# Attention with a relative bias, LayerNorm and FFN on one core: three weight scales, a value bound from sums on ScalarE, a longer PSUM group, four fp32 visits

## The chip, the cores and the metric

The kernel runs on one core of a Trainium2 chip. The metric is the device time of one execution in microseconds (us). PE is TensorE, DVE is VectorE, ACT is ScalarE, POOL is GpSimd and SP is the engine that issues most DMAs; PEld is the loading of weights into TensorE.

## The reference

```python
# q, k, v: (4, 8, 576, 64); w1: (1, 32); w2: (32, 8)
scores = (1 / 8) * q @ k^T
rel    = |i - j|;  x = log1p(rel) / log1p(max(i, 1))
bias   = relu(x * w1 + b1) @ w2                    # (576, 576, 8), the same for every batch
attn   = softmax(scores + bias);  o = attn @ v
# o is laid out as (4, 576, 512)
xn  = (o - mean) / sqrt(var + 1e-6) * g_ln
out = o + relu(xn @ w_ch1) @ w_ch2                 # 512 -> 2048 -> 512
```

All inputs and the output are fp32.

## The kernel before, in words

**Units and visits.** The attention work is cut into 144 units. A unit is one head of 128 query rows (or, in the four tail visits, two heads of the last 64 rows). Units of one batch and one row block make a visit; there are 20 visits in the order of the table `ORD`: two tail visits (units 0 to 7), then (1, 0), (0, 0), (2, 0), (3, 0) with units 8 to 39, two more tail visits (40 to 47), and twelve visits of eight units. Visit (2, 0) holds units 24 to 31.

**One unit.** PE computes the scores in fp32 into PSUM (`sps`, line 394). One DVE instruction adds the bias tile `ldb` and takes the row maximum (line 418). ACT computes the exponential and its row sum (line 422). Then there are two ways to get the product with v:

- In a visit that stands in the set `NAT`, PE transposes the fp32 probabilities in five matmuls (`ptm`, `ptl`, lines 440 and 441), ACT copies them out of PSUM (lines 442 and 443), and PE multiplies with the raw fp32 values `vf` (line 490; line 507 in a tail visit).
- Otherwise ACT rounds the probabilities to fp16 (line 427), DVE computes the fp16 remainder (lines 446 and 448), a transposing DMA of SP turns both (line 451), and PE multiplies 14 times with the split values `v` (line 461).

The split values need a scale per batch and pair of heads: `v_max` takes the largest magnitude of `vf` on DVE (line 344), writes it to DRAM and reads it back to all partitions by two DMAs (`vmx`, `vall`, lines 348 and 350); `fin` reduces that on DVE (line 354) and rounds to a power of two; `split_v` makes the two fp16 halves (lines 369 and 372). When that happens follows from `uv`, the first unit of a batch that is not in a `NAT` visit.

**Weights.** The FFN weights arrive as 64-bit integers in 32 pieces (16 blocks f of 128 hidden columns, two matrices). DVE decodes each piece in three instructions (lines 612, 615, 617), PE adds up a Gram matrix per group of blocks (`gram`, line 626), `w_scale` makes a scale per group from it (lines 631, 633, 127 to 133, 637, 640), and `split_w` cuts each piece into two fp16 halves, one instruction on ACT (line 652) and one on DVE (line 655). A group is four blocks f, as `GROUPS` says.

**FFN.** It works on 18 row blocks k of 128 rows. A job is one row block with one group: 48 matmuls into `hps` (line 678), a ReLU split on ACT (line 683) and DVE (line 686), 12 matmuls into `y` (line 706), and one DVE instruction that adds `y`, scaled, to the row block x (line 717). Jobs are taken when their weights are split and their rows are normalised (`next_fs`); the variable `mbank` spreads them over the units.

**What sets the order.** A Python loop over the unit number u writes the steps; after it a scheduler puts the instructions of each engine in a fixed order when the program is built. Each engine then works its list off in order and waits where something is not there. Buffers come from pools: `ps_h` (one buffer, tag `h`) holds `hps`, and `ps_y` (one buffer each of tags `y0` and `y1`) holds `y` and `ptm`, or `gram` and some of the bias.

Of the kernel before, what the change touches and what calls it, by code (L numbers as in the profile page):

```python
# [22 lines left out]
def kernel(  # L23
# [50 lines left out]
    cb_sb = const.tile([128, 5], F32)  # L74
    one_sb = const.tile([2, 128], F32)
    gs_sb = const.tile([128, 512], F32)
    GROUPS = ((0, 4), (4, 8), (8, 12), (12, 16))
    NG = len(GROUPS)
    GOF = [g for g, (lo, hi) in enumerate(GROUPS) for _ in range(lo, hi)]
    half2 = const.tile([128, 2], F32)  # L80
    gram = {}
# [15 lines left out]
    ]  # L97
    vmx = [dram.tile([512], F32, name=f"vmx{b}") for b in range(NB)]
    wslot = [wp.tile([128, 1024], F32, name=f"w{f}") for f in range(NF - 1)]
# [129 lines left out]

    NAT = {(0, 4), (1, 4), (1, 0), (0, 0), (2, 0)}  # L230

# [109 lines left out]
    def v_max(b, g):  # L341
        if g == 0:
            vam[b] = small.tile([128, 4], F32, tag="vam", name="vam")
        red = V.tensor_reduce(out=vam[b][:, g:g + 1], in_=vraw[b, g], op=ALU.max, axis=AX.X,
                              apply_absolute_value=True)
        after(red, ttri[max(ttri)])
        if g == 3:
            SY.dma_start(out=vmx[b].rearrange("(p g) -> p g", g=4), in_=vam[b])
            all_ = ep.tile([128, EW], F32, tag="e", name="vall")[:, 0:512]
            SY.dma_start(out=all_, in_=vmx[b].partition_broadcast(128))  # L350

            def fin():
                ar = small.tile([128, 4], F32, tag="var", name="var")
                V.tensor_reduce(out=ar, in_=all_.rearrange("p (a g) -> p g a", g=4), op=ALU.max,
                                axis=AX.X)
                vsc[b] = small.tile([128, 4], F32, tag="vs", name="vs")
                pow2(ar, vsc[b], None)
                c8[b] = small.tile([128, NH], F32, tag="c8", name="c8")
                V.tensor_scalar(out=c8[b].rearrange("p (a b) -> p a b", b=2),
                                in0=vsc[b].unsqueeze(2).to_broadcast([128, 4, 2]),  # L360
                                scalar1=E_SCALE, scalar2=None, op0=ALU.mult)

            defer(lambda: defer(fin))

# [264 lines left out]
    def w_scale(g):  # L629
        f0, f1 = GROUPS[g]  # L630
        V.tensor_reduce(out=winv[:, g], in_=gram[g][:, 0:256].rearrange("p (a b) -> p a b", a=2),
                        op=ALU.max, axis=AX.X)
        G.tensor_tensor(out=winv[:, g], in0=winv[:, g], in1=half2, op=ALU.pow)

        def fin():
            wm = part_max(winv[:, g], 2, gram[g][:, 256:512])
            V.tensor_scalar(out=wred[:, g], in0=wm, scalar1=2.0 ** -5, scalar2=1e-20,
                            op0=ALU.mult, op1=ALU.max)
            pow2(wred[:, g], ws[:, g], winv[:, g])
            V.tensor_scalar(out=ycs[:, g:g + 1], in0=winv[:, g, 0:1], scalar1=winv[:, g, 1:2],  # L640
                            scalar2=ginv, op0=ALU.mult, op1=ALU.mult)
            wspl.extend((ff, ii) for ff in range(f0, f1) for ii in range(2))

        defer(fin)
# [46 lines left out]
    yq = []  # L691
    ydone = {}

    def ffn_w2(k, fs, hh):
        nt = len(blocks[k])
        n = 128 * nt
        g = GOF[fs[0]]
        f0, f1 = GROUPS[g]
        if fs[0] == f0:
# [8 lines left out]
        if fs[-1] == f1 - 1:  # L708
            for t in range(nt):
                yq.append((k, g, t, yps[k][t]))  # L710

    def ffn_y():
        while yq:
            k, g, t, y = yq.pop(0)
            b, c = tiles[blocks[k][t]]
            x = xt[b, c].rearrange("p a d -> p (a d)")
            V.scalar_tensor_tensor(out=x, in0=y, scalar=ycs[:, g:g + 1], in1=x,  # L717
                                   op0=ALU.mult, op1=ALU.add)
            ydone[k, t] = ydone.get((k, t), 0) + 1
            if ydone[k, t] == NG:  # L720
                if c < 4:
                    SY.dma_start(out=out[b, c * 128:c * 128 + 128, :], in_=x)
                else:
                    SY.dma_start(out=out[b:b + 2, 512:576, :], in_=x)

    jobs = [(k, g) for k in range(NBL) for g in range(NG)]
    cur_job = []
# [6 lines left out]
    def next_fs(u):  # L734
        if not cur_job:
            navail = sum(1 for a in avail_at if a <= u)
            for j in jobs:
                k, g = j
                if blocks[k][-1] < navail and wready_at.get(g, 1 << 30) <= u:
                    jobs.remove(j)  # L740
                    nf = 4 // len(blocks[k])
                    f0, f1 = GROUPS[g]
                    cur_job.extend((k, range(f, f + nf)) for f in range(f0, f1, nf))
                    break
# [41 lines left out]
    V.memset(one_sb, 1.0)  # L786
    V.memset(half2, 0.5)
    bias_setup()
# [42 lines left out]
    while u < NU + 6 or jobs or cur_job or pend or yq:  # L831
# [30 lines left out]
        for fn in todo.pop(u, []):  # L862
            fn()
        for g, (f0, f1) in enumerate(GROUPS):
            if wdone[0] >= 2 * f1 and g not in wready_at:
                wready_at[g] = u
        if u < NU + 9:
# [88 lines left out]
```

## Time and profile before

| | us |
|---|---|
| three runs | 700.3, 701.18, 702.73 |
| their median | 701.18 |
| the profiled execution | 697.11 |
| its span (first to last instruction) | 695.3 |
| PE busy in the span | 655.0 (94%) |
| DVE busy | 472.6 (68%) |
| ACT busy | 387.1 (56%) |

The profile shows one execution. It was 4.07 us shorter than the median of the runs, and 1.8 us of it lie outside the span. Durations below are read from that execution. A row of the timeline shows when an instruction (or a run of equal ones, with its count) started, how long it took, and in brackets how long its engine had been idle before and what ended that.

### The profile page before, as it was taken

To read this page: it belongs to the slowest core of one execution; us is meant where nothing else is said; L and a number is where in the kernel's file an instruction comes from. 1 tells how busy PE (TensorE), PEld (TensorE's weight loads), DVE (VectorE), ACT (ScalarE), POOL (GpSimd) and SP (SyncE) were. 2 spreads that over 40 slices of the span, in tenths; PEclk is the share of its full clock that TensorE was granted. 3 is DMA by queue.
4 is the path that set the end of the run, shared out by engine and by line. 5 is a ranking of instruction groups with operands and counts; after the bars stand their busy time and mean duration, and the time that the engine had idled before them with its cause. 6 is when DMAs were issued, how large, how long until landed. Compare 5 with 4: busy or idle time off the path is not lost.

```text
span 695.3 us, 18932 instructions
## 1 busy us (share of the span) xinstructions
PE 655.0 (94%) x7836; PEld 456.3 (66%) x7836; DVE 472.6 (68%) x1074; ACT 387.1 (56%) x762; POOL 81.8 (12%) x152
## 2 busy tenths in 40 slices
PE   6685888999999999999989999999999999999997
PEld 4343675786646676676657766766677677677774
DVE  6368989878237876869686766667676775767422
ACT  5765454647657745757585576767554554544110
POOL 3202132110000011101010110101000110000000
PEclk9888899789999999999999999999999999999999
DMA  8998794611238898886888978888896876738100
GB/s 311 284 402 310 248 311 152 187 49 35 66 85 183 153 261 161 171 181 146 169 158 188 234 166 163 169 159 185 166 242 138 173 145 136 131 70 131 35 17 15
DMA packets 180457, 116.17 MB, mean 167 GB/s; under 512 B 156180, under 2 KB 156308, under 8 KB 180372
## 3 DMA queue, kind: packets, MB, share of 16 engines
q1 hardware_dynamic: 169860, 79.96, 53.7%
q0 software_dynamic: 8640, 31.20, 14.2%
q10 hardware_dynamic: 1872, 3.81, 1.7%
q8 instruction: 61, 1.00, 0.6%
q14 instruction: 24, 0.20, 0.1%
HBM read 61.56 MB, written 15.64 MB: 111 GB/s over the span
## 4 chain that ended last, share of the span: by engine, by line
PE 67%; DMA 13%; DVE 11%; ACT 4%; issue 3%; SPq 1%; DVEq 0%; ACTq 0%
PE hps L678 24%; PE y L706 22%; PE sps L394 8%; PE xps L461 6%; DMA w<-in_w_ch_dram 4%; PE bps L182 3%; DMA ldb<-nb 2%; PE xps L490 2%; DMA nb<-ev 2%; DVE t L418 2%; DMA vall<-vmx 2%; DMA pt<-e 1%; DVE e L446 1%; DVE w L655 1%; DVE w L617 1%
## 5 line engine op out<-in xcount | busy, mean ns | idle before, releaser
L678 PE MATMUL hps<-xT,w 128*128 128x128 f16 x3240 | 195.9, 220 | 1.0 <-DVE w L655 0.8
L706 PE MATMUL y<-w,hh 128*128 128x512 f16 x810 | 188.3, 380 | 0.8 <-DVE x L717 0.8
L678 PEld LDWEIGHTS <-w 128*128 128x128 f16 x3240 | 185.3, 99 | 5.6 <-issue 1.8
L422 ACT ACTIVATE t<-t,m 128x576 f32<-128x576 f32 x144 | 110.8, 770 | 92.4 <-DVE m L418 92.1
L706 PEld LDWEIGHTS <-hh 128*128 128x128 f16 x864 | 79.9, 98 | 89.1 <-issue 3.8
L418 DVE CUSTOM_DVE_ANT_0 t<-sps,ldb 128x576 f32<-128x576 f32 x144 | 105.9, 750 | 22.8 <-DMA nb<-ev 7.6
L683 ACT ACTIVATE hh<-hps 128x512 f16<-128x512 f32 x72 | 42.8, 594 | 131.3 <-PE hps L678 125.8
L446 DVE SCALAR_TENSOR_TENSOR e<-t,e 128x512 f16<-128x512 f32 x112 | 77.1, 689 | 50.7 <-ACT e L427 50.7
L394 PE MATMUL sps<-kf,qf 64*128 64x288 f32 (+1 forms) x640 | 99.5, 444 | 8.6 <-DVE m L418 8.2
L686 DVE SCALAR_TENSOR_TENSOR hh<-hps,hh 128x512 f16<-128x512 f32 x72 | 49.6, 689 | 68.3 <-ACT hh L683 68.2
L461 PEld LDWEIGHTS <-pt 128*128 128x128 f16 (+1 forms) x1680 | 56.3, 100 | 40.9 <-issue 29.3
L427 ACT ACTIVATE e<-t 128x576 f16<-128x576 f32 x112 | 73.5, 675 | 2.4 <-DMA pt<-e 0.8
L717 DVE SCALAR_TENSOR_TENSOR x<-y,ycs,x 128x512 f32<-128x512 f32 x72 | 53.7, 746 | 25.6 <-PE y L706 25.6
L394 PEld LDWEIGHTS sps<-kf,qf 64*128 64x128 f32 (+1 forms) x640 | 49.3, 179 | 31.9 <-DVE m L418 8.5
L461 PE MATMUL xps<-v,pt 128*128 128x64 f16 (+1 forms) x1680 | 65.2, 194 | 2.8 <-DVE x L497 2.6
L292 POOL DMA_DIRECT2D kf<-in_k_s_dram x56 | 31.3, 560 | 115.6 <-PE sps L394 91.3
L161 ACT ACTIVATE r<-psi_sb,par_sb 128x448 f32<-128x448 f32 (+23 forms) x72 | 40.8, 615 | 6.2 <-DMA nb<-ev 3.5
L305 POOL DMA_DIRECT2D qf<-in_q_main_dram x32 | 18.0, 563 | 192.7 <-PE sps L394 167.9
L490 PE MATMUL xps<-vf,pt 128*128 128x64 f32 (+1 forms) x240 | 37.5, 290 | 0.0
L490 PEld LDWEIGHTS xps<-vf,pt 128*128 128x128 f32 (+1 forms) x240 | 33.5, 204 | 5.4 <-issue 2.7
L188 ACT ACTIVATE ev<-bps,cb_sb,par_sb 128x144 f32<-128x144 f32 (+27 forms) x48 | 26.0, 592 | 16.8 <-PE bps L182 16.8
L182 PE MATMUL bps<-r,nw_sb 128*32 128x448 f32 (+24 forms) x200 | 28.1, 494 | 0.7 <-ACT ev L188 0.5
(108 smaller groups left out, 599.3 us busy)
## 6 DMA issues: line engine op xcount, KB each, us to landing
kf<-in_k_s_dram POOLq DMA_DIRECT2D x56, 288.0 KB, 4.5
w<-in_w_ch_dram SPq DMA_DIRECT2D x23, 512.0 KB, 7.2
ldb<-nb SPq DMA_DIRECT2D x32, 288.0 KB, 4.7
qf<-in_q_main_dram POOLq DMA_DIRECT2D x32, 256.0 KB, 4.4
nb<-ev SPq DMA_DIRECT2D x24, 296.0 KB, 3.4
vf<-in_v_p_dram POOLq DMA_DIRECT2D x16, 320.0 KB, 7.1
out_dram<-x SPq DMA_DIRECT2D x18, 256.0 KB, 2.6
wend<-in_w_ch_dram SPq DMA_DIRECT2D x7, 512.0 KB, 6.4
```

Of the source, the lines that this page charges most:

```text
L182: T.matmul(out=flat[32 * s:32 * s + 32, a:b], lhsT=nw2_sb, rhs=rs[s][:, a:b], start=True, stop=True)
L394: T.matmul(out=o, lhsT=l, rhs=kk, start=True, stop=True, tile_position=(64 * hf, 64 * e))
L418: ttri[u] = V.tensor_tensor_reduce(out=halves(t), in0=ps[:, :, 0:HS], in1=halves(bias), scale=-0.125, scalar=3e38, op0=ALU.add, op1=ALU.mi ...
L422: S.activation(t, t, AF.Exp, bias=m, scale=-1.0, accum_out=l8[b, c][:, h:h + 1])
L427: S.activation(e16[:, 0:SEQ], t, AF.Copy, scale=E_SCALE)
L446: V.scalar_tensor_tensor(out=e16[:, 640:1152], in0=t[:, 0:512], scalar=E_SCALE, in1=e16[:, 0:512], op0=ALU.mult, op1=ALU.subtract)
L461: T.matmul(out=o, lhsT=p[:, m], rhs=v[:, j, a, :], start=(i == 0), stop=(i == len(ops) - 1))
L490: T.matmul(out=o[:, h, :], lhsT=p[0:n, 128 * j:128 * j + 128], rhs=vf[0:n, j], start=(j == 0), stop=(j == 4))
L678: T.matmul(out=h[:, idx * n:idx * n + n], lhsT=w[:, wo + kk * 128:wo + kk * 128 + 128], rhs=xT[k][:, xo + kk, 0:n], start=(i == 0), stop=( ...
L686: V.scalar_tensor_tensor(out=hh[:, 1], in0=h, scalar=0.0, in1=hh[:, 0], op0=ALU.max, op1=ALU.subtract)
L706: T.matmul(out=yps[k][t], lhsT=hh[:, a, o:o + 128], rhs=w[:, wo:wo + 512], start=(f == f0 and i == 0), stop=(f == f1 - 1 and i == 2))
L717: V.scalar_tensor_tensor(out=x, in0=y, scalar=ycs[:, g:g + 1], in1=x, op0=ALU.mult, op1=ALU.add)
```

## The change: four edits in one diff

- `GROUPS` has three groups instead of four: blocks f 8 to 15 share one scale, made when all eight are decoded. The three scales for `y` are used accordingly.
- For row blocks k of 4 and above, the `y` matmuls of f 8 to 15 (two jobs) add up in one PSUM tile, and x is updated once for both. For k below 4 each of the four jobs still updates x by itself.
- The bound for v is no longer a maximum. ACT sums the magnitudes of `vf` along each partition (`Abs` with an accumulated output), PE adds the 128 partial sums with a matmul by ones into a `ps_h` tile (`vps`), and DVE multiplies by 2^-13. The two DMAs through DRAM are gone.
- `NAT` loses visit (2, 0), so its eight units take the fp16 way, and `uv[2]` becomes 24 instead of 44: the values of batch 2 are loaded, bounded and split some 20 units sooner.

```diff
-    GROUPS = ((0, 4), (4, 8), (8, 12), (12, 16))
+    GROUPS = ((0, 4), (4, 8), (8, 16))
...
-    NAT = {(0, 4), (1, 4), (1, 0), (0, 0), (2, 0)}
+    NAT = {(0, 4), (1, 4), (1, 0), (0, 0)}
...
-        red = V.tensor_reduce(out=vam[b][:, g:g + 1], in_=vraw[b, g], op=ALU.max, axis=AX.X,
-                              apply_absolute_value=True)
+        sq = e16p.tile([128, 1152], F16, tag="e16", name="vab").bitcast(BF16)[:, 0:640]
+        red = S.activation(sq, vraw[b, g], AF.Abs, accum_out=vam[b][:, g:g + 1])
         after(red, ttri[max(ttri)])
         if g == 3:
-            SY.dma_start(out=vmx[b].rearrange("(p g) -> p g", g=4), in_=vam[b])
-            all_ = ep.tile([128, EW], F32, tag="e", name="vall")[:, 0:512]
-            SY.dma_start(out=all_, in_=vmx[b].partition_broadcast(128))
+            ps = ps_h.tile([128, 512], F32, tag="h", name="vps")
+            T.matmul(out=ps[:, 0:4], lhsT=one_sb, rhs=vam[b], start=True, stop=True)
+            ar = small.tile([128, 4], F32, tag="var", name="var")
 
             def fin():
-                ar = small.tile([128, 4], F32, tag="var", name="var")
-                V.tensor_reduce(out=ar, in_=all_.rearrange("p (a g) -> p g a", g=4), op=ALU.max,
-                                axis=AX.X)
+                V.tensor_scalar(out=ar, in0=ps[:, 0:4], scalar1=2.0 ** -13, scalar2=None, op0=ALU.mult)
...
-            defer(lambda: defer(fin))
+            defer(fin)
...
-        f0, f1 = GROUPS[g]
+        f0, f1 = GROUPS[g] if k >= 4 else (fs[0], fs[-1] + 1)
...
-                yq.append((k, g, t, yps[k][t]))
+                yq.append((k, g, t, yps[k][t], f1 == NF))
...
-            ydone[k, t] = ydone.get((k, t), 0) + 1
-            if ydone[k, t] == NG:
+            if last:
...
-    jobs = [(k, g) for k in range(NBL) for g in range(NG)]
+    jobs = [(k, qq) for k in range(NBL) for qq in range(4)]
...
-                    f0, f1 = GROUPS[g]
-                    cur_job.extend((k, range(f, f + nf)) for f in range(f0, f1, nf))
+                    cur_job.extend((k, range(f, f + nf)) for f in range(4 * g, 4 * g + 4, nf))
...
-        for g, (f0, f1) in enumerate(GROUPS):
-            if wdone[0] >= 2 * f1 and g not in wready_at:
-                wready_at[g] = u
+        for qq in range(4):
+            if wdone[0] >= 8 * qq + 8 and qq not in wready_at:
+                wready_at[qq] = u
```

The change moves instructions on every engine, since the scheduler starts anew. Line numbers of the new program are 3 or 4 lower.

PE, before, in units 26 and 27 of visit (2, 0): `t_2279` and `t_2348` are fp32 probabilities, `par_sb` holds the identity, `vf` the raw values.

```order
L440 MATMUL ptm_2355<-par_sb_109,t_2279 128x128 x4
L441 MATMUL ptl_2402<-par_sb_109,t_2348 64x128
L182 MATMUL bps_2594<-r_2573,nw2_sb_111 32x368
L182 MATMUL bps_2594<-r_2575,nw2_sb_111 32x368
L394 MATMUL sps_2649<-kf_2040,qf_2042 128x288 x2
L182 MATMUL bps_2594<-r_2577,nw2_sb_111 32x368
L182 MATMUL bps_2594<-r_2579,nw2_sb_111 32x368
L440 MATMUL ptm_2401<-par_sb_109,t_2348 128x128 x4
L490 MATMUL xps_2062<-vf_1458,pt_2354 128x64 x5
```

PE, after, where the first unit of that visit begins its product: `pt_1846` came from the transposing DMA, `v_1536` is a split value tile.

```order
L675 LDWEIGHTS w10_139
L675 MATMUL hps_1986<-xT_1095,w10_139 128x128
L458 LDWEIGHTS pt_1846
L458 MATMUL xps_1934<-v_1536,pt_1846 128x64
L458 LDWEIGHTS pt_1846
```

The five transposes and five fp32 products of a unit have left PE's list for these units, and 14 fp16 products stand there.

PE, before, at the first FFN matmuls that use weight block 8 (`w8`):

```order
L626 LDWEIGHTS wend_148
L626 MATMUL gram_1423<-wend_148 128x128
L490 MATMUL xps_1491<-vf_167,pt_1557 128x64 x4
L678 LDWEIGHTS w8_141
L678 MATMUL hps_1628<-xT_1091,w8_141 128x128
```

PE, after, at the same FFN matmuls; `vps` is the matmul by ones for batch 3:

```order
L702 MATMUL y0_1869<-w7_136,hh_1777 128x512
L348 MATMUL vps_1817<-vam_1580,one_sb_113 128x4
L487 MATMUL xps_1486<-vf_165,pt_1786 128x64
L675 LDWEIGHTS w8_137
L675 MATMUL hps_1986<-xT_1095,w8_137 128x128
```

Before, these FFN matmuls stand ahead of the scores of unit 26; now they stand behind the first two jobs of the next row block, behind the scores of unit 30, and right behind `vps`, whose PSUM buffer they take over.

DVE, before, between line 418 of unit 28 and of unit 29, where the last group of weights is split (`vs_1952` is the value scale of batch 3):

```order
L640 TENSOR_SCALAR ycs_119<-winv_118,ginv_122 128x1
L372 SCALAR_TENSOR_TENSOR v_2614<-vf_1511,vs_1952,v_2614 128x10x64
L655 SCALAR_TENSOR_TENSOR w12_145<-w13_146,ws_117,w12_145 128x512 x2
L686 SCALAR_TENSOR_TENSOR hh_1887<-hps_1838,hh_1887 128x512
L655 SCALAR_TENSOR_TENSOR w13_146<-w14_147,ws_117,w13_146 128x512 x2
L717 SCALAR_TENSOR_TENSOR x_1436<-y0_1921,ycs_119,x_1436 128x512
L497 TENSOR_TENSOR x_1967<-xps_1491,rl_1964 128x512
L655 SCALAR_TENSOR_TENSOR w14_147<-wend_148,ws_117,w14_147 128x512 x2
```

DVE, after, between the same two units:

```order
L637 TENSOR_SCALAR ycs_119<-winv_118,ginv_122 128x1
L652 SCALAR_TENSOR_TENSOR w8_137<-w9_138,ws_117,w8_137 128x512
L713 SCALAR_TENSOR_TENSOR x_1437<-y0_1821,ycs_119,x_1437 128x512
L652 SCALAR_TENSOR_TENSOR w8_137<-w9_138,ws_117,w8_137 128x512
L652 SCALAR_TENSOR_TENSOR w9_138<-w10_139,ws_117,w9_138 128x512 x2
L652 SCALAR_TENSOR_TENSOR w10_139<-w11_140,ws_117,w10_139 128x512 x2
L652 SCALAR_TENSOR_TENSOR w11_140<-w12_141,ws_117,w11_140 128x512 x2
L713 SCALAR_TENSOR_TENSOR x_1437<-y0_1869,ycs_119,x_1437 128x512
L352 TENSOR_SCALAR var_1819<-vps_1817 128x4
L494 TENSOR_TENSOR x_1904<-xps_1486,rl_1901 128x512
L652 SCALAR_TENSOR_TENSOR w12_141<-w13_142,ws_117,w12_141 128x512
```

The splits of blocks 8 to 11 have moved here from units 22 to 24, ahead of those of block 12 and up, and the reading of `vps` stands behind them; before, no value scale is read here.

## Rows read from the trace of the kernel before

**Rows 1.** Page, busy time, share and instructions of each engine
```profile
PE 655.0 (94%) x7836; PEld 456.3 (66%) x7836; DVE 472.6 (68%) x1074; ACT 387.1 (56%) x762; POOL 81.8 (12%) x152
```

**Rows 2.** Windows: stretch, length, busy PE, PEld, DVE, ACT, POOL, PEclk, DMA share, GB/s
```profile
144.00:181.30 37.30, 36.84 (x322) 24.65 (x322) 27.94 (x65) 23.52 (x46) 4.35 (x8) 1.00 0.22 61
181.30:237.30 56.00, 54.20 (x550) 35.58 (x549) 31.01 (x71) 38.11 (x77) 2.29 (x4) 1.00 0.58 120
300.00:380.00 80.00, 76.08 (x951) 51.11 (x948) 60.73 (x136) 53.90 (x106) 9.46 (x17) 1.00 0.77 162
380.00:640.00 260.00, 260.00 (x3375) 185.01 (x3372) 178.77 (x416) 145.64 (x288) 26.62 (x52) 1.00 0.80 161
```

**Rows 3.** Timeline of PE in visit (2, 0): fp32 transposes and products
```profile
182.01 0.30 PE L441 MATMUL ptl<-par_sb,t 128*64 128x128 f32 x1
182.24 0.43 PE L490 MATMUL xps<-vf,pt 64*128 64x64 f32 x2
...
186.70 0.61 PE L440 MATMUL ptm<-par_sb,t 128*128 128x128 f32 x4
187.15 1.36 PE L490 MATMUL xps<-vf,pt 128*128 128x64 f32 x10
188.44 0.89 PE L182 MATMUL bps<-r,nw_sb 128*32 128x416 f32 x4
```

**Rows 4.** Timeline of PE in a later visit: fp16 products
```profile
303.96 0.58 PE L461 MATMUL xps<-v,pt 128*128 128x64 f16 x14
304.38 2.84 PE L678 MATMUL hps<-xT,w 128*128 128x128 f16 x48
```

**Rows 5.** Groups of instructions by line over the span
```profile
L717 DVE SCALAR_TENSOR_TENSOR x<-y,ycs,x 128x512 f32<-128x512 f32 x72 | 53.7, 746 | 25.6 <-PE y L706 25.6
L461 PE MATMUL xps<-v,pt 128*128 128x64 f16 (+1 forms) x1680 | 65.2, 194 | 2.8 <-DVE x L497 2.6 <-DMA pt<-e 0.3
L655 DVE SCALAR_TENSOR_TENSOR w<-w,ws,w 128x512 f16<-128x512 f32 x28 | 20.5, 742 | 1.8 <-ACT w L652 1.7
L369 ACT ACTIVATE v<-vf,vs 128x640 f16<-128x640 f32 x16 | 13.2, 824 | 10.7 <-DVE vs L105 6.4 <-DVE v L372 4.3
```

**Rows 6.** Timeline of DVE where it waits for the value maximum
```profile
309.28 1.06 DVE L354 TENSOR_REDUCE var<-vall 128x4 f32<-128x512 f32 x1 [4.33 <-DMA vall<-vmx]
...
344.46 1.07 DVE L354 TENSOR_REDUCE var<-vall 128x4 f32<-128x512 f32 x1 [3.28 <-DMA vall<-vmx]
```

**Rows 7.** Timeline of PE at the end of the span
```profile
688.60 2.10 PE L706 MATMUL y<-w,hh 128*128 128x512 f16 x9 [0.84 <-DVE x L717]
```

**Rows 8.** Timeline of PE at a scale of weights
```profile
157.65 0.38 PE L133 MATMUL gram<-pdg,one_sb 2*128 2x2 f32 x2
157.96 2.85 PE L678 MATMUL hps<-xT,w 128*128 128x128 f16 x48
160.65 2.75 PE L706 MATMUL y<-w,hh 128*128 128x512 f16 x12
```

**Rows 9.** Timeline of DVE around the split of the last group
```profile
154.52 0.75 DVE L418 CUSTOM_DVE_ANT_0 t<-sps,ldb 128x576 f32<-128x576 f32 x1
...
160.29 0.27 DVE L640 TENSOR_SCALAR ycs<-winv,ginv 128x1 f32<-128x1 f32 x1
161.28 1.41 DVE L655 SCALAR_TENSOR_TENSOR w<-w,ws,w 128x512 f16<-128x512 f32 x2
169.08 0.75 DVE L655 SCALAR_TENSOR_TENSOR wend<-wend,ws 128x512 f16<-128x512 f32 x1 [0.47 <-ACT wend L652]
170.41 0.75 DVE L418 CUSTOM_DVE_ANT_0 t<-sps,ldb 128x576 f32<-128x576 f32 x1
```

**Rows 10.** Windows of 3 us around a fall of the clock
```profile
126.00:129.00 3.00, 1.78 (x16) 1.57 (x14) 3.00 (x8) 2.90 (x7) 0.53 (x1) 1.00 1.13 182
129.00:132.00 3.00, 3.00 (x14) 2.06 (x14) 3.00 (x7) 1.41 (x4) 0.54 (x1) 0.56 0.71 259
141.00:144.00 3.00, 3.00 (x30) 2.93 (x27) 0.28 (x1) 0.60 (x1) 0.00 (x0) 0.67 0.00 0
```

More of the change, by code (lines that the diff above doesn't have):

```diff
@@ L74 @@
     cb_sb = const.tile([128, 5], F32)
-    one_sb = const.tile([2, 128], F32)
+    one_sb = const.tile([128, 128], F32)
     gs_sb = const.tile([128, 512], F32)
-    GROUPS = ((0, 4), (4, 8), (8, 12), (12, 16))
+    GROUPS = ((0, 4), (4, 8), (8, 16))
     NG = len(GROUPS)
     GOF = [g for g, (lo, hi) in enumerate(GROUPS) for _ in range(lo, hi)]
-    half2 = const.tile([128, 2], F32)
+    half4 = const.tile([128, 4], F32)
     gram = {}
@@ L97 @@
     ]
-    vmx = [dram.tile([512], F32, name=f"vmx{b}") for b in range(NB)]
     wslot = [wp.tile([128, 1024], F32, name=f"w{f}") for f in range(NF - 1)]
@@ L632, in w_scale @@
                         op=ALU.max, axis=AX.X)
-        G.tensor_tensor(out=winv[:, g], in0=winv[:, g], in1=half2, op=ALU.pow)
+        G.tensor_tensor(out=winv[:, g], in0=winv[:, g], in1=half4[:, 0:2], op=ALU.pow)
         def fin():
@@ L691 @@
     yq = []
-    ydone = {}
     def ffn_w2(k, fs, hh):
@@ L709, in ffn_w2 @@
             for t in range(nt):
-                yq.append((k, g, t, yps[k][t]))
+                yq.append((k, g, t, yps[k][t], f1 == NF))
     def ffn_y():
         while yq:
-            k, g, t, y = yq.pop(0)
+            k, g, t, y, last = yq.pop(0)
             b, c = tiles[blocks[k][t]]
@@ L786 @@
     V.memset(one_sb, 1.0)
-    V.memset(half2, 0.5)
+    V.memset(half4, 0.5)
     bias_setup()
```

## The prediction

> **What bounds the kernel now.** I read the page's first part, then the windows by stage, then the timeline of PE and DVE at the places that the change touches, and last what DVE waited for. PE is busy for 655.0 of 695.3 us [rows 1], and the windows say where the rest is: from 380 to 640 us PE is busy for 260.00 of 260 us, while DVE has 178.77 and ACT 145.64; from 144 to 237.3 us, the stretch with visit (2, 0), it is busy for 91.04 of 93.3 us; from 300 to 380 us it lacks 3.92 us [rows 2]. So from about 144 us on the end is set by how much work stands on PE's list, and relief for DVE or ACT is worth nothing in itself. Ahead of 144 us PE waits for others, and its clock falls at times, once as in [rows 10].
>
> [...] I trust the row that says PE leaves no gap; if only the weight-load share (71%) of a saved matmul microsecond came back, the first term below would be 8.8 instead of 12.4 us and the sum 11.1 instead of 14.7 us.
>
> **The change, part by part.**
>
> *Visit (2, 0) in fp16.* One fp32 unit takes from start to start 187.15 - 186.70 = 0.45 us for four transposes, 182.24 - 182.01 = 0.23 us for the fifth, and 188.44 - 187.15 = 1.29 us for the ten records of its product, 1.97 us together [rows 3]. One fp16 unit takes 304.38 - 303.96 = 0.42 us [rows 4]. Eight units: 8 x (1.97 - 0.42) = 12.4 us less on PE, in a stretch where PE has no gaps, so it counts in full. The busy mean gives 65.2 / 1680 x 14 = 0.54 us for an fp16 unit [rows 5], which makes the saving 11.4 us; reading the fp32 unit by its durations (0.61 + 1.36 + 0.30 = 2.27 us) makes it 14.8 us. I take 12.4, the start-to-start figure, which is what PE's list moves by. For this DVE gets two more instructions per unit and ACT one in place of two copies; DVE has 31.01 of 56.00 us in use there and ACT 38.11 [rows 2], so they are hidden while the stretch stays longer than about 40 us. SP gets eight more transposing DMAs; they stand behind the last weight loads and ahead of the first bias writes, in a stretch where the DMA share is 0.22 [rows 2], so I cost them at nothing; if that cover failed, each would hold its unit's product by the time of a DMA, and later work on PE would fill the gap.
>
> *The value bound.* DVE loses 16 reductions and four more over `vall`, and above all it no longer stands still for a round trip through DRAM: 4.33 and 3.28 us in the stretch of 300 to 380 us [rows 6]. That stall reaches PE late, as scores whose PSUM isn't free and products whose probabilities aren't there, and PE's missing 3.92 us lie in just this stretch [rows 2]. I take 3.5 us of it as won. The bounds are 0 (another wait takes its place) and 3.92 us. ACT takes over the sums: the nearest row is a 128x640 pass of ACT at 824 ns [rows 5]; 16 of them are 13.2 us of ACT, plus a reading of the accumulator each, spread over 16 units, and ACT is busy for 53.90 of 80 us there [rows 2]: hidden. The matmul by ones occurs four times; the nearest row is the pair of tiny fp32 matmuls at 157.65, 0.31 us until the next one starts [rows 8]. At half of that each, 0.6 us, it costs about what the dropped fourth weight scale gives back (0.31 us and one transpose). I count both as 0, with 1 us to either side. What is late next, where the stall goes: DVE's read of `vps` waits for PE, which by then has passed the scores two units ahead, so I expect no gap there.
>
> *One PSUM group for f 8 to 15.* 14 of the 18 row blocks lose one update of x, 14 x 0.746 = 10.4 us of DVE [rows 5]. In 380 to 640 us that is worth nothing, for PE has no gap to give. At the end it is: PE waits 0.84 us for the update of the third quarter before it may begin the fourth [rows 7], and in a shared group there is nothing to wait for. I take 0.8 us.
>
> *Three weight scales.* This is where the change adds a wait. Before, w8 to w11 were split in units 22 to 24; now their scale is known only when block 15 is decoded. DVE's list then runs: scale, eight splits of w8 to w11 with two updates of x among them, and then the read of `vps`. PE's list has the `hps` matmuls on w8 right behind `vps`, in the same single PSUM buffer, so they start no earlier than that read. Behind them on PE stand the first fp16 products and the scores of unit 31 and on; ACT's ReLU and DVE's line 418 wait for those. In the trace of before eight splits, mixed with other work, took from 161.28 to 169.83 us, 8.6 us [rows 9], and the scale is known 5.8 us after line 418 of unit 28 begins (160.29 - 154.52). So PE may go on about 14 us after that. What PE has of its own in that time, on its list between the scores of unit 28 and `vps`: one `hps` job (2.69 us from start to start) and two `y` jobs of 2.75 us [rows 8], two groups of bias matmuls at 0.89 us and an fp32 half unit of 1 us [rows 3], and the scores of two units, for which I put 1.4 us: some 12 us in all. That leaves a stall of about 2 us. The bounds: 0 if PE still carries work from before, 7 us if it has already caught up when line 418 of unit 28 begins. I take 2 us. The whole DVE stretch between units 28 and 29 stays about as long as it was, 15.9 us [rows 9], as the value splits of batch 3 leave it (three of them) and four more weight splits come in at 742 ns.
>
> *Sum.* -12.4 - 3.5 - 0.8 + 2.0 = -14.7 us, from 697.11 us (the profiled execution, 695.3 us of span and 1.8 us around it) to 682.4 us. The runs shown have their median 4.07 us higher, at 701.18; taken from there the forecast is 686.5 us.
>
> **The rivals.**
>
> *The clock stays up as well.* From 129 us on the granted clock is 0.56, then half, and it is back only in the window that ends at 144 us [rows 10]: some 14 us at 1.2 instead of 2.4 GHz, which cost about 7 us of PE work. It fell after a window in which PE was busy for 1.78 of 3 us. If the new order leaves no such hole there, the gain is 14.7 + 7 = 21.7 us, 679.5 us. For it: units 24 to 28 carry less DVE work than before. Against: up to unit 22 nothing gets easier, and the `vps` of batch 2 puts a wait ahead of a job there too.
>
> *The clock falls once more.* PE now has less to do between 144 and 180 us and waits behind the split of w8. If that wait grows to 7 us and the clock then halves for 14 us as it did, 5 + 7 us are lost: a gain of 2.7 us, 698.5 us. The Trainium skill (TensorE: Matmul & The Clock Gate, section HAM oscillation) says just this, that gaps on PE throttle it and the work behind them starts cold; the trace agrees, with PE idle for 1.22 of 3 us ahead of the fall [rows 10]. Against it: with 36.84 of 37.30 us busy [rows 2] PE has much to lose before it shows holes of that size.
>
> *Half of the weights behind one event* (slower). All work on w8 to w15 now hangs on the last decoded piece. Until then PE has only four jobs with the first eight weight blocks for the two row blocks that are ready. If the scale comes so late that PE stands still at w8 for more than 14.7 + 2 + 2.1 = 18.8 us, the kernel is slower than before by more than can be told from no change. For it: in the trace the last scale is known only at 160.29 us [rows 9]. Against: PE's list puts all work that is free ahead of w8, so the stall would have to be nine times my estimate. With 23 us of stall: 701.18 - 16.7 + 23 = 707.5 us.
>
> *The DVE relief was the point.* If DVE were what holds PE back in the long stretch too, 14 updates of x would come on top: up to 10 us, 676 us. The window with 260.00 of 260 us speaks against it; I give it no chance of its own.
>
> **How the numbers follow.** Forecast (a gain of 8 to 19 us): 0.60; the clock stays up: 0.15; the clock falls once more: 0.18; slower: 0.07. The ends of the terms give 14.8 + 3.9 + 0.8 + 1 + 7 = 27.5 us of gain at most and, with no gain but 11.4 us, 7 us of stall, 1 us for the tiny matmuls and 7 us of clock, 3.6 us of loss. The range for 8 in 10 leaves out the ends of both: 677 to 698 us. A measurement tells about 0.3%, 2.1 us, from no change. Faster by more: all of the first two cases and half of the third, 0.84; within: most of the other half and a little of the last, 0.08; slower: 0.08.
>
> **What would show it.** In the new profile: no `ptm` after unit 23, and visit (2, 0) about 12 us shorter on PE between the scores of units 24 and 40; PE without gaps from 300 us on, and no wait of DVE for a value bound above 1 us; the last two `y` jobs back to back; a gap on PE ahead of the first `hps` on w8 of some 2 us, ended by DVE. PE's busy time should fall by 11 to 13 us and its idle time by 2 or 3. It is wrong if the span before unit 40 is as long as it was with PE idle in it, if the granted clock is below 0.9 in a stretch between 144 and 240 us, or if PE gets gaps in the long stretch.

## The result and the profile after

The changed kernel took 691.57 us (median of four runs, 690.12 to 693.24) beside 701.05 us for the kernel before, of which there was one run more by then: a ratio of 0.9862 with a 95% interval of 0.9834 to 0.9891. A repeat of it in the study below gave 0.9913 (0.9867 to 0.9959). So it is faster, by about 9.5 us by the first runs and about 6 us by the repeat's ratio, where 14.7 us were forecast. Executions of one kernel differ by more than that: on one chip those of the kernel before lay between 690.02 us (mean granted clock 0.980) and 709.45 us (0.958). Hence single profiles are trusted for places and waits more than for totals. The ratios in this document leave out executions more than 1.5% above the fastest of their kernel and the medians do not, so a kernel can have the lower median and still a ratio above 1.

The profiled execution took 691.74 us, 690.0 us of it in the span. First the page's line of busy times, which answers to [rows 1]:

```profile
PE 643.2 (93%) x7833; PEld 441.2 (64%) x7833; DVE 453.9 (66%) x1051; ACT 395.4 (57%) x786; POOL 81.4 (12%) x151
```

PE's busy time fell from 655.0 to 643.2 us, 11.8 us less. But the span is only 5.3 us shorter: PE's idle time rose by 6.5 us, from 695.3 - 655.0 = 40.3 to 690.0 - 643.2 = 46.8 us, where the prediction has it fall by 2 or 3. In the profile of the repeat (span 689.8 us) PE is busy for 645.9 us and idle for 43.9. The windows of the same stretches as in [rows 2] (stretch, length, busy PE, PEld, DVE, ACT, POOL, granted clock, DMA share, GB/s), and two more, over 80 to 180 and 180 to 380 us:

```profile
80.00:180.00 100.00, 85.92 (x807) 63.17 (x809) 81.38 (x188) 67.90 (x142) 15.66 (x26) 0.97 0.65 169
180.00:380.00 200.00, 194.31 (x2501) 128.96 (x2496) 133.20 (x314) 129.78 (x264) 20.94 (x39) 0.99 0.90 169
...
144.00:181.30 37.30, 34.50 (x366) 22.91 (x364) 29.02 (x67) 30.66 (x56) 5.17 (x8) 0.97 0.50 102
181.30:237.30 56.00, 52.20 (x621) 32.94 (x620) 35.06 (x83) 35.88 (x74) 4.60 (x9) 0.98 0.83 150
300.00:380.00 80.00, 78.27 (x980) 52.87 (x977) 55.94 (x132) 54.75 (x111) 10.23 (x18) 1.00 0.91 166
380.00:640.00 260.00, 260.00 (x3344) 181.12 (x3343) 169.09 (x393) 142.33 (x281) 25.77 (x50) 1.00 0.77 155
```

From 300 us on it went in part as forecast: PE lacks 1.73 us where it lacked 3.92 us, and nothing from 380 to 640 us. These 1.73 us are one gap, and another wait stands behind it: ACT waits 3.21 us for a bias tile, so that the ReLU split `hh`, which PE needs, comes late.

```profile
351.95 0.62 ACT L160 ACTIVATE r<-psi_sb,par_sb 128x385 f32<-128x385 f32 x1 [3.21 <-DMA nb<-ev]
...
353.82 2.84 PE L675 MATMUL hps<-xT,w 128*128 128x128 f16 x48 [1.73 <-DVE hh L683]
```

Over 180 to 380 us PE idles for 5.69 us, and for 5.71 us in the same window of the kernel before, so what was won behind 300 us was lost ahead of it. From 80 to 180 us PE idles for 14.08 us, where the kernel before has 6.25, at a lower clock:

```profile
80.00:180.00 100.00, 93.75 (x784) 70.23 (x785) 82.19 (x186) 56.36 (x117) 17.72 (x30) 0.91 0.53 157
180.00:380.00 200.00, 194.29 (x2437) 130.63 (x2436) 138.62 (x312) 129.19 (x256) 20.25 (x37) 1.00 0.75 160
```

The places, in the timeline of PE of the changed kernel (start, duration, in brackets the idle time before and what ended it):

```profile
99.92 2.85 PE L675 MATMUL hps<-xT,w 128*128 128x128 f16 x48 [3.24 <-DMA xT<-x]
...
105.25 0.41 PE L623 MATMUL gram<-w 128*128 128x128 bf16 x4 [1.57 <-DVE w L614]
...
138.00 0.40 PE L623 MATMUL gram<-wend 128*128 128x128 bf16 x4 [1.82 <-DVE wend L614]
...
162.69 0.28 PE L348 MATMUL vps<-vam,one_sb 128*128 128x4 f32 x2
162.90 0.43 PE L487 MATMUL xps<-vf,pt 64*128 64x64 f32 x2
163.76 1.78 PE L675 MATMUL hps<-xT,w 128*128 128x128 f16 x29 [0.43 <-DVE var L352]
165.38 0.98 PE L458 MATMUL xps<-v,pt 128*128 128x64 f16 x28
...
170.61 0.58 PE L458 MATMUL xps<-v,pt 128*128 128x64 f16 x14 [2.37 <-DMA pt<-e]
...
234.61 0.73 PE L458 MATMUL xps<-v,pt 128*128 128x64 f16 x14 [2.08 <-DMA pt<-e]
235.15 4.34 PE L675 MATMUL hps<-xT,w 128*128 128x128 f16 x48
...
680.24 4.70 PE L702 MATMUL y<-w,hh 128*128 128x512 f16 x21
684.77 0.81 PE L702 MATMUL y<-wend,hh 128*128 128x512 f16 x3
```

The gap that I had priced, the one ahead of the first `hps` on w8 (163.76), is 0.43 us. The gaps that I had not priced are ended by DMAs (a transposed x, transposed probabilities) and by DVE's decoding, which itself waited 5.40 and 3.69 us for weight pieces. At 235.15 a job takes 4.34 us where 2.85 is usual: the clock had fallen after two gaps of 1.21 and 2.08 us, as the windows show. At the end the last two `y` jobs run without a gap, where [rows 7] had 0.84 us.

Windows of 3 us, answering to [rows 10], and two around a later fall of the clock:

```profile
126.00:129.00 3.00, 2.73 (x18) 1.68 (x17) 2.65 (x5) 2.79 (x8) 1.27 (x2) 1.00 0.87 190
129.00:132.00 3.00, 2.67 (x23) 2.26 (x23) 2.63 (x5) 2.24 (x6) 0.00 (x0) 1.00 0.94 246
138.00:141.00 3.00, 3.00 (x22) 2.64 (x22) 3.00 (x11) 1.62 (x4) 0.00 (x0) 0.72 0.03 5
141.00:144.00 3.00, 3.00 (x27) 2.49 (x25) 3.00 (x9) 2.46 (x6) 0.00 (x0) 0.50 0.01 3
231.00:234.00 3.00, 1.54 (x18) 0.51 (x16) 2.12 (x5) 0.87 (x2) 1.60 (x3) 1.00 0.91 193
234.00:237.00 3.00, 2.39 (x32) 2.39 (x33) 1.26 (x5) 2.12 (x4) 0.00 (x0) 0.65 1.11 382
```

The half-clock stretch has moved from 129 to 138 us and is shorter, and a second one has come at 234 us.

DVE, between the scale of the last group and line 415 of unit 29, answering to [rows 9]:

```profile
155.51 0.27 DVE L637 TENSOR_SCALAR ycs<-winv,ginv 128x1 f32<-128x1 f32 x1
...
157.02 2.29 DVE L652 SCALAR_TENSOR_TENSOR w<-w,ws,w 128x512 f16<-128x512 f32 x3
159.54 2.96 DVE L652 SCALAR_TENSOR_TENSOR w<-w,ws,w 128x512 f16<-128x512 f32 x4 [0.24 <-ACT w L649]
...
163.56 0.15 DVE L352 TENSOR_SCALAR var<-vps 128x4 f32<-128x4 f32 x1
...
168.40 0.76 DVE L415 CUSTOM_DVE_ANT_0 t<-sps,ldb 128x576 f32<-128x576 f32 x1
```

`vps` is read 8 us after the scale is known, and the next scores are taken 4.8 us later, about as forecast.

### The profile page after: what moved, and what is told of

Read it like the earlier page. It is cut to its first block, busy times and chain, and to the rows that moved or that the text cites. A ratio compares the mean times of both kernels' runs of the same rounds, so it can differ in the third digit from the quotient of the medians.

```text
span 690.0 us, 18930 instructions
## 1 busy us (share of the span) xinstructions
PE 643.2 (93%) x7833; PEld 441.2 (64%) x7833; DVE 453.9 (66%) x1051; ACT 395.4 (57%) x786; POOL 81.4 (12%) x151
## 4 chain that ended last, share of the span: by engine, by line
PE 60%; DMA 1%; ACT 1%; DVE 1%; issue 0%; ACTq 0%
PE hps L675 22%; PE y L702 21%; PE sps L391 8%; PE xps L458 7%; PE bps L181 2%; DMA pt<-e 1%; DMA nb<-ev 1%; ACT e L424 0%; ACT r L160 0%; ACT t L419 0%; DVE hh L683 0%; DVE e L443 0%; DVE v L369 0%; DVE x L713 0%; DVE u L553 0%
## 5 line engine op out<-in xcount | busy, mean ns | idle before, releaser
L675 PE MATMUL hps<-xT,w 128*128 128x128 f16 x3240 | 197.9, 221 | 6.0 <-DMA xT<-x 3.2
L443 DVE SCALAR_TENSOR_TENSOR e<-t,e 128x512 f16<-128x512 f32 x120 | 82.8, 690 | 80.8 <-ACT e L424 80.7
L424 ACT ACTIVATE e<-t 128x576 f16<-128x576 f32 x120 | 80.9, 678 | 7.9 <-DMA pt<-e 5.5
L458 PEld LDWEIGHTS <-pt 128*128 128x128 f16 (+1 forms) x1792 | 58.5, 100 | 37.4 <-issue 28.2
L458 PE MATMUL xps<-v,pt 128*128 128x64 f16 (+1 forms) x1792 | 70.4, 194 | 6.1 <-DMA pt<-e 6.1
L713 DVE SCALAR_TENSOR_TENSOR x<-y,ycs,x 128x512 f32<-128x512 f32 x58 | 43.4, 749 | 33.6 <-PE y L702 33.4
L419 ACT ACTIVATION_READ_ACCUMULATOR t<-t,m 128x1 f32 x144 | 27.0, 188 | 0.0
L445 DVE SCALAR_TENSOR_TENSOR e<-t,e 128x64 f16<-128x64 f32 x120 | 26.3, 219 | 0.0
```

The lines of the kernel that those rows point to most:

```text
L419: S.activation(t, t, AF.Exp, bias=m, scale=-1.0, accum_out=l8[b, c][:, h:h + 1])
L424: S.activation(e16[:, 0:SEQ], t, AF.Copy, scale=E_SCALE)
L443: V.scalar_tensor_tensor(out=e16[:, 640:1152], in0=t[:, 0:512], scalar=E_SCALE, in1=e16[:, 0:512], op0=ALU.mult, op1=ALU.subtract)
L458: T.matmul(out=o, lhsT=p[:, m], rhs=v[:, j, a, :], start=(i == 0), stop=(i == len(ops) - 1))
L675: T.matmul(out=h[:, idx * n:idx * n + n], lhsT=w[:, wo + kk * 128:wo + kk * 128 + 128], rhs=xT[k][:, xo + kk, 0:n], start=(i == 0), stop=( ...
```

## The experiments

Three edits (I count the three scales and the shared PSUM tile as one, the weight edit) can be made in eight ways. Two are the kernels before and after; the other six were run, then variants that take single parts apart. Medians in us, and ratios to the kernel before on the same chip with their 95% intervals:

| fp16 visit | value bound | weight edit | median | ratio |
|---|---|---|---|---|
| - | - | - | 698.02, 699.47, 695.54 (three chips) | 1 |
| yes | - | - | 697.23 | 1.0044 (1.0000 to 1.0088) |
| - | yes | - | 700.47 | 1.0052 (1.0010 to 1.0094) |
| - | - | yes | 718.58 | 1.0265 (1.0165 to 1.0365) |
| - | yes | yes | 708.92 | 1.0141 (1.0071 to 1.0211) |
| yes | - | yes | 706.39 | 1.0128 (1.0063 to 1.0193) |
| yes | yes | - | 684.86; again 683.63 | 0.9819 (0.9760 to 0.9879); 0.9843 (0.9787 to 0.9899) |
| yes | yes | yes | 691.62 | 0.9913 (0.9867 to 0.9959) |

**The fp16 visit alone.**

```diff
-    NAT = {(0, 4), (1, 4), (1, 0), (0, 0), (2, 0)}
+    NAT = {(0, 4), (1, 4), (1, 0), (0, 0)}
```

> The kernel before with one edit: visit (2, 0) takes the fp16 way. Theory A (that edit is the gain, and it also brings the new waits for DMAs, since it moves the four value loads of batch 2 some seven units earlier and adds eight transposing DMAs): PE busy falls by about 10 us (fp32 products, `ptm` and `ptl` of eight units go: 9.7 + 3.7 + 6.1 + 2.5 us by the groups of lines, 5.2 us of fp16 products come: 17 us by summed durations, which overlap; 12 from start to start), PE idle rises by 3 to 7 us, and the time is 693 to 697 us. Theory B (the new waits come from the weight scales or from the value bound): idle as before, 688 to 690 us. Rival C (the early value scale through DRAM now stops DVE ahead of unit 24, where PE waits for DVE anyway): 697 to 703 us.

697.23 us: no gain. This is the top end of theory A, and rival C gives the same time, so the time does not part them. In the profiled execution (701.39 us) PE is busy for 654.8 us, as before, at a mean clock of 0.958 against 0.973. Adding up busy time times (1 - granted clock) over windows of 1 us, the clock costs 25.3 us there against 15.4 us before; without it PE's work (its busy time less what the clock costs) is 10.0 us less. In this execution the work is saved and given back in clock and in idle time (44.8 against 40.3 us). It is 4 us above the median and has the lowest clock of the twelve, so its 25.3 us are at the high end. In 300 to 380 us alone, where DVE waits 4.42 and 5.06 us for the value maximum, PE is idle for 7.32 us (before: 3.92).

**The value bound alone.**

```diff
-        red = V.tensor_reduce(out=vam[b][:, g:g + 1], in_=vraw[b, g], op=ALU.max, axis=AX.X,
-                              apply_absolute_value=True)
+        red = S.activation(sq, vraw[b, g], AF.Abs, accum_out=vam[b][:, g:g + 1])
...
+            T.matmul(out=ps[:, 0:4], lhsT=one_sb, rhs=vam[b], start=True, stop=True)
```

> The kernel before with one edit: the value bound from magnitudes summed on ScalarE and added by a matmul. By my forecast 3.5 us less (697.5 us, PE without idle time in 300 to 380 us); rival: another wait takes the place of the one removed and the time stays within 1 us of before (700 to 702 us).

700.47 us, 1.0010 to 1.0094 of before: the rival, if anything worse. In 300 to 380 us PE's idle time does fall, from 3.92 to 1.20 us. But ahead of it another wait has grown, one that DVE has for a bias tile:

```profile
209.45 0.76 DVE L415 CUSTOM_DVE_ANT_0 t<-sps,ldb 128x576 f32<-128x576 f32 x1 [8.56 <-DMA nb<-ev]
```

It was 6.11 us in the kernel before. PE idles for 3.71 us between 200 and 220 us (1.70 before), and its clock is 0.50 from 215 to 220 us. That is only a part of it: over the span idle time is 1.2 us less than before, the clock costs 2.0 us more, and PE's work, with the same matmuls and eight tiny ones, is 4.4 us more in the new order.

**The weight edit alone.**

```diff
-    GROUPS = ((0, 4), (4, 8), (8, 12), (12, 16))
+    GROUPS = ((0, 4), (4, 8), (8, 16))
...
-        f0, f1 = GROUPS[g]
+        f0, f1 = GROUPS[g] if k >= 4 else (fs[0], fs[-1] + 1)
```

> The kernel before with the third edit: three weight scales, and one PSUM group for blocks 8 to 15 of the row blocks 4 and up. By my forecast -0.8 us at the end and +0 to +7 us where PE waits for w8: 700 to 704 us. Rival (the splits of w8 to w11 leave units 22 to 24, so that the hole ahead of the half-clock stretch closes): clock above 0.9 between 129 and 143 us and 696 to 699 us.

718.58 us. Both expectations fail: by the ratio it is 18 us slower. Its DVE and PE where a value maximum comes back late:

```profile
313.51 1.07 DVE L354 TENSOR_REDUCE var<-vall 128x4 f32<-128x512 f32 x1 [4.06 <-DMA vall<-vmx]
...
322.81 0.68 DVE L686 SCALAR_TENSOR_TENSOR hh<-hps,hh 128x512 f16<-128x512 f32 x1
...
323.55 4.32 PE L678 MATMUL hps<-xT,w 128*128 128x128 f16 x48 [2.09 <-DVE hh L686]
```

DVE waits 4.06 us, works off what has piled up, and the ReLU split `hh`, which frees PE's `hps` buffer, comes so late that PE stands still for 2.09 us and then runs the job at half clock (4.32 us). That suggested that the edits work jointly, and the next four kernels test it.

**Value bound and weight edit, visit (2, 0) in fp32.** Against the changed kernel:

```diff
-    NAT = {(0, 4), (1, 4), (1, 0), (0, 0)}
+    NAT = {(0, 4), (1, 4), (1, 0), (0, 0), (2, 0)}
```

> Two edits together: value bound and weight groups; visit (2, 0) stays in fp32. Theory J (the edits work jointly: what made the weight groups alone slow were DVE's waits for the value maximum through DRAM, 3.87, 4.06 and 6.11 us in that run, behind which the split `hh` stood that PE waited for, 3.07, 2.09 and 2.60 us, each followed by a stretch at half clock): without that round trip the gaps go, PE idle in 300 to 380 us falls from 5.9 to below 2.5 us with the clock at 1.00, and the time is 694 to 702 us. Rival (each edit has its own price, and the prices add up): 718.6 + 2.4 = 721 us.

708.92 us: between the two. The gaps behind the maximum are gone (PE idles 2.95 us in 300 to 380 us instead of 5.93, where less than 2.5 was expected), and about 9 us come back, not 17 to 25. New gaps of 1.81, 3.83 and 2.11 us, all ended by transposed probabilities, stand at 234 to 244 us.

**Fp16 visit and weight edit, value maximum through DRAM.** Against the changed kernel:

```diff
-        red = S.activation(sq, vraw[b, g], AF.Abs, accum_out=vam[b][:, g:g + 1])
+        red = V.tensor_reduce(out=vam[b][:, g:g + 1], in_=vraw[b, g], op=ALU.max, axis=AX.X,
+                              apply_absolute_value=True)
...
+            SY.dma_start(out=vmx[b].rearrange("(p g) -> p g", g=4), in_=vam[b])
+            SY.dma_start(out=all_, in_=vmx[b].partition_broadcast(128))
```

> Two edits together: fp16 visit and weight groups; the value bound stays a maximum through DRAM. Theory J: the waits of DVE for the maximum are there again (one for each batch, 3 to 6 us), PE loses 4 to 10 us more than in the changed kernel in idle time and clock in 300 to 380 us, time 697 to 708 us. Rival (the fp16 visit by itself mends the weight groups): 690 to 695 us. Rival (prices add up): 697.2 + 20.6 = 718 us.

706.39 us, as theory J has it. One window shows it:

```profile
300.00:380.00 80.00, 67.91 (x815) 45.53 (x813) 54.52 (x122) 48.59 (x96) 7.59 (x15) 0.98 0.74 142
```

12.09 us of idle time here, where the changed kernel has 1.73; five of the gaps (2.10, 1.26, 1.35, 1.36, 1.93 us) are waits for `hh`.

**Fp16 visit and value bound, four weight groups.** Against the changed kernel:

```diff
-    GROUPS = ((0, 4), (4, 8), (8, 16))
+    GROUPS = ((0, 4), (4, 8), (8, 12), (12, 16))
...
-        f0, f1 = GROUPS[g] if k >= 4 else (fs[0], fs[-1] + 1)
+        f0, f1 = GROUPS[g] if k >= NBL else (fs[0], fs[-1] + 1)
```

> Two edits together: fp16 visit and value bound; four weight groups and an update of x for each as before. Theory J: the fp16 visit alone lost 7.3 us of idle time and 1.5 us of clock in 300 to 380 us; without the round trip that falls to below 2.5 us, so 690 to 694 us, and the weight groups add nothing or a loss. Rival (the weight groups carry part of the gain, by 14 updates of x less on DVE): 695 to 700 us.

684.86 us, and 683.63 on another chip. That is 5 us below the expected 690 to 694 us, and faster than the changed kernel: the weight edit is a loss of 6.8 us (691.62 - 684.86, same chip).

Its repeat, and that of the changed kernel, without an edit:

> The two edits that gain once more, on the chip of the other three: 0.982 of the kernel before, 683 to 688 us. If the weight edit's price of 6.8 us is real, it lies 4 to 9 us below the changed kernel's 691.6; if it is above 690, that price was chance.

> The changed kernel itself once more, beside the kernels of two edits on the same chip: 0.986 of the kernel before by its first runs, so about 688 us if that kernel is again at 698. If it is above 0.993, the first runs had luck with the clock.

The repeat of two edits falls where it was expected. That of the changed kernel, at 0.9913, lies above the expected 0.986 and below the 0.993 that was to mean luck with the clock. So the gain of the whole change is that of two edits, and as built here the third takes about half of it away. In the windows of the profiled executions, the kernel of two edits and its repeat:

```profile
80.00:180.00 100.00, 96.81 (x859) 70.85 (x859) 88.22 (x211) 73.35 (x152) 18.48 (x27) 0.90 0.62 173
```

```profile
80.00:180.00 100.00, 92.08 (x856) 66.64 (x855) 87.51 (x207) 70.83 (x148) 18.41 (x27) 0.95 0.66 177
```

PE idles for 3.19 and 7.92 us here, against 14.08 and 10.91 us in the two profiles of the changed kernel; from 180 to 380 us all four agree (5.7 to 6.5 us idle). But the granted clock is 0.90 and 0.95 here, against 0.97 in both profiles of the changed kernel, and what a lower clock costs has to be set beside the idle time. Counted as for the fp16 visit alone, over whole spans, in us:

| profile | span | PE idle | cost of the clock | PE's work |
|---|---|---|---|---|
| before | 695.3 | 40.3 | 15.4 | 639.5 |
| two edits | 681.8 | 37.6 | 20.1 | 624.1 |
| two edits, repeat | 681.3 | 41.8 | 14.8 | 624.7 |
| changed | 690.0 | 46.8 | 12.4 | 630.8 |
| changed, repeat | 689.8 | 43.9 | 16.2 | 629.7 |

Between the two pairs the span differs by 8.3 us: idle time holds 5.7 of them, the clock gives 3.2 back, and 5.8 us are PE's work. PE issues the same matmuls but three, in another order, and is busy with them for longer. So the gaps from 80 to 180 us are one part of what is missing, and not the larger one. Why the new order keeps PE busy for longer no run here shows.

**Which part of the weight edit.** First the shared PSUM tile is taken back, with the three scales kept:

```diff
-        f0, f1 = GROUPS[g] if k >= 4 else (fs[0], fs[-1] + 1)
+        f0, f1 = GROUPS[g] if k >= NBL else (fs[0], fs[-1] + 1)
```

> The changed kernel with three scales, but each job updates x by itself again (no PSUM tile over two jobs). My forecast: 0.8 us more than the changed kernel, 692.4 us. Theory L (the late scale alone costs what the weight edit costs, 6.8 us between 684.9 and 691.6): 691 to 693.5 us. Rival (holding the PSUM tile over two jobs is what costs): 685 to 688 us. Rival (14 fewer updates of x are worth their 10.4 us of DVE): 698 to 702 us.

692.46 us (0.9959, 0.9930 to 0.9988): theory L. The shared tile isn't what costs: PE's work is 630.3 us, as in the changed kernel. What 14 more updates of x cost is too little to tell from these runs. The gap ahead of the last job is back, to the hundredth:

```profile
682.08 2.10 PE L702 MATMUL y<-w,hh 128*128 128x512 f16 x9 [0.84 <-DVE x L713]
```

Then the late scale is made worse:

```diff
-    GROUPS = ((0, 4), (4, 8), (8, 16))
+    GROUPS = ((0, 4), (4, 16))
```

> The suspected cost raised: two scales, blocks 0 to 3 and 4 to 15, so that the splits of w4 to w7 too wait for the last decoded piece (and from row block 4 on three jobs add up in one PSUM tile). Theory L (weights split late: DVE has the splits in one piece ahead of line 415 of unit 29, 0.75 us each, and PE has fewer jobs to fill its gaps from 95 to 180 us): 8 more splits late, line 415 of unit 29 some 5 us later than the 168.4 us of the changed kernel, PE idle before 180 us higher by 3 us or more, time 696 to 708 us. Rival (the cost is one of chance in the order): 686 to 694 us.

696.14 us (0.9992, 0.9958 to 1.0026), the lower end of theory L: 3.7 us above the kernel with three scales and no shared tile, on the same chip, and 4.5 us above the changed kernel on another. It also holds the PSUM tile over three jobs, which no other kernel here does. PE idles for 16.58 us in the window:

```profile
80.00:180.00 100.00, 83.42 (x756) 59.10 (x755) 81.28 (x185) 68.22 (x145) 15.15 (x25) 0.93 0.72 188
```

One half of theory L falls here, though. Line 415 of unit 29 starts at 157.21 us, not 5 us later than 168.40 but 11 us earlier: the scheduler spread the splits among the units, and the kernel is slower all the same. So here it isn't the run of splits in one piece that costs. Nor does the amount of FFN work in that stretch tell the price: from 80 to 180 us PE issues 36 matmuls into `y` with two scales, 60 in both profiles of the changed kernel, 64 and 72 with four scales, but 65 with three scales and no shared tile, which is 8.8 us slower than the kernel with 64 (692.46 and 683.63, same chip).

**The value loads of batch 2, later.** The change moved the bound and the split of batch 2 by 20 steps, but its loads by seven only, from step 16 to step 9; this edit puts the loads back, with bound and split two to four steps later to match. In the changed kernel and in that of two edits:

```diff
-    vneed = {0: -5, 1: 1, 2: min(uv[2] - 15, ustart[2, 0] - 8),
+    vneed = {0: -5, 1: 1, 2: ustart[2, 0] - 8,
...
-            at(u0 - 11 + g, lambda b=b, g=g: v_max(b, g))
-            at(u0 - 4 + 2 * g if b else u0 - 4 + 2 * g, lambda b=b, g=g: split_v(b, g))
+            at(u0 - (7 if b == 2 else 11) + g, lambda b=b, g=g: v_max(b, g))
+            at(u0 - 2 + g if b == 2 else u0 - 4 + 2 * g, lambda b=b, g=g: split_v(b, g))
```

> The changed kernel with the value loads of batch 2 issued at steps 16 to 19 as in the kernel before, the sums of magnitudes at 17 to 20 and the splits at 22 to 25; the order of SP's DMAs stays. Theory A (the early value loads delay the transposing DMA of xT and the weight loads around 84 to 103 us): PE's wait of 3.24 us for xT near 96.7 us and DVE's 5.4 us for a weight near 100 us shrink to below 1.5 us each, and the time falls by 3 to 5 us, to 687 to 689 us. Rival (these DMAs are slow whatever the value loads do, or PE catches up later): within 1.5 us of 691.6. Second rival (the value loads of two batches now stand together and the split of batch 2 comes too late for unit 24): 692 to 696 us.

689.97 us (0.9909, 0.9865 to 0.9953), no different from the repeat's 0.9913. The local part of theory A holds for PE: in 80 to 100 us it is now busy for 19.70 of 20 us and does not wait for xT (DVE still waits 1.74 us for a weight, where less than 1.5 was expected). But the time isn't kept, since from 100 to 120 us it now lacks 6.10 us, 2.22 of them for `hh`.

> The two edits that gain (fp16 visit, value bound; four weight groups), and the value loads of batch 2 at steps 16 to 19 as in the kernel before. With the later loads the changed kernel was at 690.0 beside 691.6 us of its own repeat. Theory A (early loads delay other DMAs): 682 to 684 us, beside the kernel of the two edits at 685. Rival: within 1.5 us of that kernel, or above.

688.72 us (0.9898, 0.9863 to 0.9932): some 4 to 5 us slower than without it, which neither expectation has, but for the rival's last words. A gap of 5.43 us has come at a place far from the edit:

```profile
260.39 0.96 PE L458 MATMUL xps<-v,pt 128*64 128x64 f16 x28 [5.43 <-DVE x L519]
```

DVE's instruction there stands behind a remainder that waits for ACT, which waited 5.33 us for a transposing DMA. The best version found is that of two edits, without the later loads.

The two kernels with later loads are also a fifth comparison with and without the weight edit, and here its price is gone: 0.9909 with it and 0.9898 without, on two chips, and spans of 687.5 and 687.4 us. And an edit that only moves loads, bounds and splits made the kernel of two edits 4 to 5 us slower, so such a move by itself can change the time by most of what the weight edit seems to cost.

## Why the prediction was right in sign and off in size

*The fp16 visit and the value bound* (12.4 and 3.5 us). Together they were forecast at 15.9 us and measured at ratios of 0.9819 and 0.9843, which is 12.6 and 10.9 us, each with an interval some 8 us wide. PE's busy time was to fall by 11 to 13 us: it fell by 11.8 us in the changed kernel, 9.1 us in its repeat, 10.8 and 15.5 us with the two edits alone. DVE no longer waits for a bound (its read of `vps` isn't among the waits over 1 us). The value bound's own 3.5 us did not come as idle time: in 300 to 380 us PE's gaps shrank by 1.4 to 2.2 us, a wait for a bias tile stands behind the one that is left, and over 180 to 380 us idle time is about as before. That is in good part the prediction's lower bound of 0, that another wait takes its place.

What was wrong with both terms is that I priced them apart and added up. Neither gains anything alone. The fp16 visit without the new bound leaves 7.3 to 12.1 us of idle time in 300 to 380 us, where I had counted with 3.9; the new bound without the fp16 visit runs into the wait for bias tiles and has 4.4 us more work on PE.

The Trainium skill (Perfetto Trace Analysis, section Identifying the Most-Contended Engine) calls matmul busy time no good measure of how near PE is to its limit, and names MFU (the share of the peak arithmetic rate) and the busy share of weight loads instead. By the weight-load share of the long stretch (185.01 of 260 us) the two edits would be worth 8.8 + 3.5 = 12.3 us; the runs are near that, but their intervals, 8 to 17 and 7 to 15 us, don't decide between it and 15.9.

*Three weight scales* (+2.0 us, bounds 0 to 7) is the term that was too small. I looked for the price in one place, the stall ahead of the first `hps` on w8, and worked it out as 2 us. That stall is 0.43 us. The price of the whole weight edit, the 0.8 us of the shared tile taken off, is 6.8 us (691.62 - 684.86, same chip). By the ratios it is 6 to 18 us in four comparisons, with 4.8 to 11.9 us more idle time on PE in the profiles (5.7 in the mean of the two pairs above), and about 1 us, which is nothing that these runs can tell, in the fifth, with later loads. In all five PE's work rises too, by 1.4 to 5.8 us, which the prediction had at nothing: it counted what stands on PE's list and not the order.

That the price goes with the three scales and not with the PSUM tile is shown by taking the tile back. How the late scale makes it is not shown: with two scales it isn't the run of splits; the gaps are a part, and the rest is an order in which PE is busy for longer. In the kernels with visit (2, 0) in fp32 the added idle time stands at 180 to 380 us instead. The scheduler makes a new order for every variant, and moving loads, bounds and splits alone changed the time by 4 to 5 us, so how much of the 6.8 us is chance of the order stays open.

*Blocks 8 to 15 in one PSUM tile* (-0.8 us): right in place and size, 0.84 us with and without.

*Costed at nothing, and wrong*: the transposing DMAs of visit (2, 0). I named the cover, a stretch with a DMA share of 0.22 [rows 2]. The share is now 0.50, and 0.83 in the stretch behind it, and PE waits for `pt` for 6.1 us in all. In the two profiles of the kernel of two edits it is 3.4 and 0.8 us, so the DMAs alone don't set this price. *At nothing, and no run speaks against it*: the 14 updates of x and the matmuls by ones.

*The rivals.* "The clock falls once more" happened in part: 2.08 us of waiting, then 0.65 of the clock and a job of 4.34 us. The Trainium skill's rule (TensorE: Matmul & The Clock Gate, section HAM oscillation), that gaps throttle PE and the work behind them starts cold, agrees with this trace. It is also one of the signs that I had named for being wrong, a granted clock below 0.9 between 144 and 240 us, if a stretch of 3 us counts. But the earlier half-clock stretch became shorter, and over the span the clock costs 12.4 us instead of 15.4 (16.2 in the repeat). "Half of the weights behind one event" was given 0.07 with a stall of 18.8 us as its mark; that stall did not come.

So the forecast had the sign right and the larger terms in the main. That the time lay inside the range owes something to luck: two terms were each worth nothing without the other, and the one that was too small stayed smaller than their sum.

## What to carry to other kernels

An edit that makes work wait for a later event can cost more than the stall at that event: here 0.43 us of stall went with 6.8 us of time. Idle time alone doesn't show where it went. Set beside it what the clock costs, and how long PE is busy with the same list in its new order. When several edits come in one change, price them jointly, and run them in pairs as well as alone: here two that gain nothing alone gain 11 to 13 us together, and the third took about half of it back. Where a scheduler starts anew, try an edit that you expect to be neutral as well: here one that only moved loads, bounds and splits made 4 to 5 us.

## What the runs showed that was not expected

- Granted clock and time go together across executions of the same program: over 29 runs of the kernel before on one chip the correlation is -0.82, and 0.01 of mean clock goes with 5.6 us (-0.92 and -0.81, with 5.8 and 4.6 us, on two other chips).
- After two gaps in short order, of 1.21 and 2.08 us, with PE busy for 1.54 of the last 3 us at clock 1.00, the next 3 us have 0.65, and a job of 2.85 us takes 4.34.
- PE's work, its busy time less the cost of the clock, depends on the order of its list: with the same matmuls but three it was 624.1 and 624.7 us in one order, 630.8 and 629.7 us in another.
- A transposing DMA of x issued at 84.6 us, beside loads of weights, keys, queries and values of 256 to 512 KB (medians of 7.9 to 11.3 us from issue to landing), took 15.3 us; one in the stretch from 216 to 242 us, beside transfers with medians of 3.9 to 7.5 us, took 4.8 us.
